# Chains of dependent operations split into single steps, in a new hand-written order, in an SSD and SwiGLU kernel on one core

## The chip, the cores and the metric

The kernel runs on one core of one Trainium2 chip. The core has five engines with an instruction queue each: TensorE (PE, with its weight loads shown as PEld), VectorE (DVE), ScalarE (ACT), GpSimd (POOL) and SyncE (SP, which here issues nearly all DMAs). Every engine works through its own queue in order; between engines an instruction waits on a semaphore. The metric is the device time of the program in microseconds (us), median over runs; lower is better.

## The reference

Two stages, one behind the other, all in fp32:

```python
# stage 1: x (4 batches, 8 heads, 768 steps, 32), a (4, 8, 768), B and C (4, 8, 768, 16); chunks of 32
log_a = np.log(np.clip(a, 1e-06, 1.0))
cum = np.cumsum(la, axis=-1)                       # within a chunk
L = np.exp(cum[:, :, :, None] - cum[:, :, None, :]) * causal
y_intra = (C B^T * L) x
y_inter = (C state) * exp(cum)
state = exp(sum(la)) * state + sum_j B_j x_j * exp(cum[-1] - cum_j)
# stage 2: y reshaped to 3072 tokens x 256
xn = x / sqrt(mean(x * x) + 1e-06) * rms_g
g = xn @ w_gate                                    # 256 -> 1536
silu = g / (1 + exp(-g))
val = xn @ w_val
out = (silu * val) @ w_out                         # 1536 -> 256
```

The weights of the second stage come as 64-bit floats and are turned into 32-bit ones on the chip.

## The kernel before, in words

The 3072 tokens are worked in six blocks of 512, and each block's first stage in two pairs of 128-token chunks (the pairs 0 to 11). While TensorE does the second stage of one block, the other engines prepare the first stage of the next ones. Block 0 has code of its own, since its first stage and the conversion of the weights have to be done before anything else can run.

*First stage.* A logarithm of `a`, sums of it by matmuls (`sums_of_logs`, L402; `row_sums`, L1161), and `three_parts` (L411 to L417), which splits a row of sums into three bf16 parts in four steps on DVE, each reading the one before. `mask` (L474) opens a PSUM pair with a mask, `sums` (L488, L495) adds the sums to it, and `decay` takes the exponential on ACT. `products` (L606, L613) makes `g`, C times B; `decayed` (L646 to L658) multiplies the two on DVE into `L`. `additions` (L678) gives what each chunk adds to the state, and `states` (L692 to L702) carries the state along on DVE: one masked copy for each half, then a chain of steps of 128 x 64 elements. `outputs` (L719 to L750) makes `y`. `squares` (L791, L802), `norm_sums` (L830, L834), `norm_roots` (two steps on ACT, a logarithm and an exponential) and `norm_apply` (L861, L865) do the RMS norm; `taken_out` (L812 to L821) copies `y` out of PSUM. For later pairs the decays come from rows spread by DMA (`spread`, L514), a subtraction (L520, DVE or POOL), an exponential on ACT and a triangular cut on POOL (`causal`, L507).

*Weights.* They come in 18 pieces. `fetch` issues the DMA (L182, L185) into one of six buffers; `power` (three steps on ACT, each reading the one before) makes the exponent, `mantissa` (two steps on DVE, L234 and L237) the fraction, and `weight` (L243, DVE) multiplies them into `wgv` or `wo`.

*Second stage.* For the later products gate and value come by a Strassen-like scheme of seven products (`product_gv`, L965) over sums of weights (`combine_w`, L934) and of tokens (`combine_x`, L942); ACT takes a part sum out of PSUM (`taken_gv`, the copy `p`, L971), DVE adds (`total_gv`, `c`, L977), ACT applies the silu (L215, a helper through which all activations go), DVE or POOL multiplies (`hide_gv`, `hid`, L990). The output product has a scheme of twenty products (`product_o`, L1086) over sums (`sum_h`, `combine_wo`) and totals (`total_o`, L1117, L1113). Block 0 starts with plain products (`products_early`, L889; `products_gv`, L879; `normed`, L900; `hidden`, L912; `first_projection`, L997).

Silu and the exponential or logarithm live in two tables of ACT. `functions` (L202 to L209) issues a table load each time the needed table differs from the one that is in.

*The order.* There is no scheduler: one string, `order` (from L1284), names every step of the program, as `block:kind.arguments`. The steps are emitted as the string has them, and each lands at the end of its engine's queue. `/n` picks a PSUM pair, `*n` puts n filler matmuls ahead. A step that is a chain in its helper, as `pow`, `man`, `parts`, `S`, `sq`, `yt`, `rs`, `norm`, `ex`, goes into its queue as a whole.

Of the kernel before, what the change touches and what calls it, by code (L numbers as in the profile page):

```python
# [20 lines left out]
def kernel(  # L21
# [195 lines left out]
    def power(k):  # L217
        words16, (lo, hi), dst, shape = fetched[k]
        n = shape[1] * shape[2]
        e = cvt.tile([P, n], FP32, tag="e", name="e", bufs=4)  # L220
        k16 = e.bitcast(I16)[:, n:2 * n].rearrange("p (a b) -> p a b", a=shape[1])
        g = e.rearrange("p (a b) -> p a b", a=shape[1])
        b16 = e.bitcast(I16)[:, 0:n].rearrange("p (a b) -> p a b", a=shape[1])
        activation(out=k16, in_=words16, func=AF.Relu, scale=1.0 / 16, bias=kinks[:, 0:1])
        activation(out=g, in_=k16, func=AF.Prelu, scale=-1.0, bias=kinks[:, 1:2],
                             alpha=2.0 ** -20)
        activation(out=b16, in_=g, func=AF.Prelu, scale=-2.0 ** 27, bias=kinks[:, 2:3],
                             alpha=2.0 ** -20)
        parts[k, "e"] = b16.bitcast(BF16)

    def mantissa(k):
        words16, (lo, hi), dst, shape = fetched[k]
        m = cvt.tile(shape, I32, tag="m", name="m")
        nc.vector.tensor_scalar(out=m, in0=hi, scalar1=0xFFFFF, scalar2=0x100000,  # L234
                                op0=ALU.bitwise_and, op1=ALU.bitwise_or)
        parts[k, "f"] = f = m.bitcast(FP32)
        nc.vector.scalar_tensor_tensor(out=f, in0=lo.bitcast(U32), scalar=2.0 ** -32, in1=m,  # L237
                                       op0=ALU.mult, op1=ALU.add)
# [54 lines left out]
    def whole_chunks():  # L293
        nc.vector.memset(chunk_ones, 0.0)
        for u, r in enumerate(halves):
            nc.vector.memset(chunk_ones[r, u], 1.0)
# [12 lines left out]
    def of_quarters():  # L309
        nc.vector.tensor_scalar(out=three, in0=part[:, 3:4], scalar1=-1.0, scalar2=1.0,  # L310
                                op0=ALU.mult, op1=ALU.add)
        nc.vector.tensor_scalar_add(later_part, part[:, 0:1], -1.0)
        nc.vector.tensor_scalar(out=third_part, in0=part[:, 2:3], scalar1=-1.0, scalar2=None,
                                op0=ALU.mult)
# [4 lines left out]
    def from_middle():  # L319
        nc.vector.tensor_copy(out=mid, in_=upto)  # L320
        nc.vector.tensor_scalar_add(mid[0:HC], mid[0:HC], -1.0)

    def from_middles():
        nc.gpsimd.tensor_copy(out=mid, in_=upto)
        for r in halves:
            half_of = slice(r.start, r.start + HC // 2)
            nc.gpsimd.tensor_scalar(out=mid[half_of, r], in0=mid[half_of, r], scalar1=-1.0,
                                    scalar2=None, op0=ALU.add)
        minus_mid()

    def mask16():
        for r in halves:
            nc.vector.tensor_copy(out=never16[r], in_=never[r, r])

    def kinks_of_powers():
        for k, v in enumerate((1152.0 - 7.5 / 16, 256.0, -1792.0 * 128.0)):
            nc.vector.memset(kinks[:, k:k + 1], v)
# [68 lines left out]
    def three_parts(k):  # L406
        r_ps = ps.pop(("r", k))
        room = nrm.tile([P, 4, P], FP32, tag="lead1", name="room", bufs=1)
        first, second = [room[:, k].bitcast(BF16).rearrange("p (s m) -> p s m", s=2)
                         for k in range(2)]  # L410
        nc.vector.tensor_copy(out=first, in_=r_ps)  # L411
        rest = room[:, 2:4]
        nc.vector.scalar_tensor_tensor(out=rest, in0=first, scalar=later_part, in1=r_ps,
                                       op0=ALU.mult, op1=ALU.add)
        nc.vector.tensor_copy(out=second, in_=rest)
        rows[k] = row = const.tile([P, 2, P], BF16, name="row%d" % k)
        nc.vector.scalar_tensor_tensor(out=row, in0=second, scalar=third_part, in1=rest,  # L417
                                       op0=ALU.mult, op1=ALU.add)
# [31 lines left out]
    def chunk_decays():  # L450
        activation(out=full.rearrange("p g h -> p (g h)"), in_=ps.pop("c"), func=AF.Exp)
        nc.gpsimd.tensor_tensor(out=fsel, in0=full,
# [52 lines left out]
    def causal(L):  # L505
        for r in halves:
            nc.gpsimd.affine_select(out=L[r], in_=L[r], pattern=[[0, L.shape[1]], [1, HC]],  # L507
                                    compare_op=ALU.is_ge, fill=0.0, base=0, channel_multiplier=-1)

    def spread(g):  # L510
        b, c = divmod(g, NC)
        o = (c * BH + b * NH) * HC
        for u, r in enumerate(halves):
            nc.sync.dma_start(out=pair_tile(g)[r].rearrange("p h m -> p (h m)"),  # L514
                              in_=rowv[u, o:o + NH * HC].partition_broadcast(HC))
# [8 lines left out]
    def exponential(g):  # L524
        L = pair_tile(g)
        activation(out=L, in_=L, func=AF.Exp)
        causal(L)

    def decays(g):
        subtract(g)  # L530
        exponential(g)
# [153 lines left out]
    def states(p):  # L685
        A_ps = ps.pop(("A", p))
        b, c0, chunks = chunks_of(p)
        new = ssd.tile([P, 2, 2, 2, D], FP32, tag="A", name="A")
        for u in range(2):
            n = sum(v == u for i, v in chunks)  # L690
            if n:
                nc.vector.tensor_tensor(  # L692
                    out=new[:, u, 0:n], in0=A_ps[u][:, 0:n],
                    in1=tmask.unsqueeze(1).unsqueeze(3).to_broadcast([P, n, 2, D]), op=ALU.mult)
        for i, u in chunks:
# [87 lines left out]
    def squares(p):  # L783
        blk, half = divmod(p, 2)
        if half == 0:
            sqs[blk] = nrm.tile([P, 2, TB], FP32, tag="sq", name="sq", bufs=1)
        n, tk, cols = columns_of_y(p)
        if p < 2:
            sq2 = sqs[blk][:, 1].rearrange("p (k m) -> p k m", k=2)
            activation(out=sq2, in_=ps["y", p][:, :, 0:256], func=AF.Square)  # L790
            nc.gpsimd.tensor_tensor(out=sqs[blk][:, 0, tk], in0=sq2[:, 0], in1=sq2[:, 1],  # L791
                                    op=ALU.add)
# [3 lines left out]
        for k in range(2):  # L796
            activation(out=dst[:, k, 0], func=AF.Square,
                                 in_=y[2 * k][:, cols].rearrange("p (j m) -> p j m", j=n))
        activation(
            out=dst[:, :, 1], func=AF.Square,  # L800
            in_=ps["y pair", p][:, :, cols].rearrange("p k (j m) -> p k j m", j=n))
        nc.gpsimd.tensor_tensor(out=sqs[blk][:, 0, tk], in0=sqs[blk][:, 0, tk],  # L802
                                in1=sqs[blk][:, 1, tk], op=ALU.add)

    def taken_out(p, copy):
        blk, half = divmod(p, 2)
        if half == 0:
            yts[blk] = nrm.tile([P, 2, TB], FP32, tag="yt", name="yt", bufs=1)
        n, tk, cols = columns_of_y(p)
        if p < 2:  # L810
            for t in range(2):
                nc.vector.tensor_scalar(out=yts[0][:, t, tk], in0=ps["y", p][:, t, 0:256],  # L812
                                        scalar1=gcol[:, t:t + 1], scalar2=None, op0=ALU.mult)
# [3 lines left out]
        for k in range(2):  # L817
            copy(out=dst[:, k, 0], in_=y[2 * k][:, cols].rearrange("p (j m) -> p j m", j=n))
        pair = ps["y pair", p][:, :, cols].rearrange("p k (j m) -> p k j m", j=n)
        for r, there in zip(halves, halves[::-1]):  # L820
# [672 lines left out]
```

## Time and profile before

| what | us |
|---|---|
| median of 3 runs | 392.02 |
| the three runs | 392.02, 392.39, 391.25 |
| profiled execution: its span | 389.5 |
| busy of it: PE, DVE, ACT, POOL | 383.3, 289.8, 226.4, 152.0 |

The times hold the whole program. The span reaches from the first to the last instruction of one profiled execution. Its own time outside the span isn't listed; to the median of the runs it lacks 2.5 us. In the rows shown below, a time such as 37.87 is the start in us from the beginning of the span, followed by the duration; then the engine, the line of the kernel, the operation, output and inputs by the names of the program, and their shapes. A bracket at the end gives the idle time ahead of the instruction and what ended it. TensorE's granted clock is 1.00 over the whole span.

### The profile page before, as it was taken

To read this page: it belongs to the slowest core of one execution; us is meant where nothing else is said; L and a number is where in the kernel's file an instruction comes from. 1 tells how busy PE (TensorE), PEld (TensorE's weight loads), DVE (VectorE), ACT (ScalarE), POOL (GpSimd) and SP (SyncE) were. 2 spreads that over 40 slices of the span, in tenths; PEclk is the share of its full clock that TensorE was granted. 3 is DMA by queue.
4 is the path that set the end of the run, shared out by engine and by line. 5 is a ranking of instruction groups with operands and counts; after the bars stand their busy time and mean duration, and the time that the engine had idled before them with its cause. 6 is when DMAs were issued, how large, how long until landed. Compare 5 with 4: busy or idle time off the path is not lost.

```text
span 389.5 us, 9637 instructions
## 1 busy us (share of the span) xinstructions
PE 383.3 (98%) x3805; PEld 329.8 (85%) x3805; DVE 289.8 (74%) x612; ACT 226.4 (58%) x471; POOL 152.0 (39%) x168
## 2 busy tenths in 40 slices
PE   8999999999999999999999999999999999999996
PEld 5676478788888999888899988899888899988995
DVE  6999999997976988669594765768374577454684
ACT  2899979988767262665865234763444571345420
POOL 5022045523693455343577701364611234212231
PEclk9999999999999999999999999999999999999999
DMA  8978984474073414634336112000100001000001
GB/s 107 241 153 259 240 195 147 120 157 42 3 101 86 50 13 94 145 42 96 70 78 81 27 42 42 2 15 22 56 3 2 2 12 50 29 0 0 2 0 56
DMA packets 109940, 28.05 MB, mean 72 GB/s; under 512 B 94824, under 2 KB 103752, under 8 KB 109896
## 3 DMA queue, kind: packets, MB, share of 16 engines
q1 hardware_dynamic: 107816, 27.31, 32.8%
q8 instruction: 30, 0.49, 0.5%
q10 hardware_dynamic: 2080, 0.13, 0.4%
q14 instruction: 14, 0.11, 0.1%
HBM read 23.69 MB, written 3.74 MB: 70 GB/s over the span
## 4 chain that ended last, share of the span: by engine, by line
PE 87%; DVE 9%; issue 2%; ACT 1%; DVEq 0%; ACTq 0%
PE gate L965 29%; PE o L1086 23%; PE val L965 21%; PE o L997 5%; PE y L750 3%; PE g L613 1%; DVE wgv L243 1%; DVE m L237 1%; DVE m L234 1%; DVE hid L912 1%; PE g L606 1%; PE e L474 1%; PE y L678 1%; DVE L L652 1%; ACT yt L821 0%
## 5 line engine op out<-in xcount | busy, mean ns | idle before, releaser
L977 DVE TENSOR_TENSOR c<-val,p 128x512 f32<-128x512 f32 x99 | 67.4, 686 | 45.1 <-PE val L965 33.3
L971 ACT COPY p<-gate 128x512 f32<-128x512 f32 x99 | 56.8, 581 | 57.5 <-PE gate L965 55.4
L965 PE MATMUL gate<-tx,wgv 128*128 128x256 f32 x264 | 65.9, 381 | 0.0
L215 ACT ACTIVATE c<-c 128x256 f32<-128x256 f32 x99 | 40.0, 415 | 38.7 <-DVE c L977 38.4
L990 POOL TENSOR_TENSOR hid<-c 128x256 f32<-128x256 f32 x31 | 24.7, 800 | 87.1 <-ACT c L215 83.1
L965 PEld LDWEIGHTS gate<-tx,wgv 128*128 128x128 f32 x264 | 49.2, 190 | 7.3 <-ACT p L971 0.7
L1117 DVE TENSOR_TENSOR ob<-ob,o 128x128 f32<-128x128 f32 (+1 forms) x90 | 24.2, 298 | 21.7 <-PE o L1086 16.9
L990 DVE TENSOR_TENSOR hid<-c 128x256 f32<-128x256 f32 x68 | 34.5, 521 | 6.9 <-ACT c L215 6.7
L1086 PE MATMUL o<-two,hid 128*128 128x128 f32 x280 | 36.5, 276 | 0.1
L1086 PEld LDWEIGHTS o<-two,hid 128*128 128x128 f32 x280 | 34.5, 192 | 1.1 <-DVE hid L990 0.4
L965 PE MATMUL val<-xn,wgv 128*128 128x256 f32 x132 | 33.7, 381 | 0.0
L965 PE MATMUL val<-tx,sw 128*128 128x256 f32 x132 | 33.5, 380 | 0.0
L965 PE MATMUL val<-xn,sw 128*128 128x256 f32 x132 | 33.3, 381 | 0.0
L965 PE MATMUL gate<-tx,sw 128*128 128x256 f32 x132 | 33.1, 381 | 0.0
L965 PE MATMUL gate<-xn,wgv 128*128 128x256 f32 x132 | 32.8, 381 | 0.0
L507 POOL TENSOR_SCALAR_AFFINE_SELECT L<-L 64x512 f32<-64x512 f32 x32 | 23.6, 737 | 18.6 <-ACT L L215 17.4
L965 PEld LDWEIGHTS val<-xn,wgv 128*128 128x128 f32 x132 | 24.8, 190 | 3.5
L965 PEld LDWEIGHTS val<-tx,sw 128*128 128x128 f32 x132 | 24.8, 190 | 3.5 <-issue 0.2
L965 PEld LDWEIGHTS gate<-tx,sw 128*128 128x128 f32 x132 | 24.7, 190 | 3.5 <-ACT p L971 0.2
L965 PEld LDWEIGHTS gate<-xn,wgv 128*128 128x128 f32 x132 | 24.3, 190 | 3.4 <-DVE hid L912 0.3
L965 PEld LDWEIGHTS val<-xn,sw 128*128 128x128 f32 x132 | 24.4, 190 | 3.2 <-issue 0.2
L215 ACT ACTIVATE e<-e,kinks 128x512 f32<-128x512 int16 (+1 forms) x36 | 26.0, 722 | 1.2
(203 smaller groups left out, 717.0 us busy)
## 6 DMA issues: line engine op xcount, KB each, us to landing
L<-rowd SPq DMA_DIRECT2D x32, 128.0 KB, 3.4
xr<-in_x_dram SPq DMA_DIRECT2D x24, 128.0 KB, 3.2
wr<-in_moe_w_out_dram SPq DMA_DIRECT2D x6, 512.0 KB, 5.6
out_dram<-ob SPq DMA_DIRECT2D x24, 128.0 KB, 1.8
wr<-in_moe_w_gate_dram SPq DMA_DIRECT2D x5, 512.0 KB, 5.8
wr<-in_moe_w_val_dram SPq DMA_DIRECT2D x5, 512.0 KB
br<-in_B_dram SPq DMA_DIRECT2D x23, 64.0 KB, 2.6
dT<-rowe SPq DMA_DIRECT2D x10, 128.0 KB
```

Of the source, the lines that this page charges most:

```text
L215: nc.scalar.activation(**operands)
L234: nc.vector.tensor_scalar(out=m, in0=hi, scalar1=0xFFFFF, scalar2=0x100000, op0=ALU.bitwise_and, op1=ALU.bitwise_or)
L237: nc.vector.scalar_tensor_tensor(out=f, in0=lo.bitcast(U32), scalar=2.0 ** -32, in1=m, op0=ALU.mult, op1=ALU.add)
L507: nc.gpsimd.affine_select(out=L[r], in_=L[r], pattern=[[0, L.shape[1]], [1, HC]], compare_op=ALU.is_ge, fill=0.0, base=0, channel_multipli ...
L750: nc.tensor.matmul(out=y[2 * k + u][rows, (2 * n + i) * HC:(2 * n + i + 1) * HC], start=(k, u, rows.start) not in opened, stop=True, skip_ ...
L965: nc.tensor.matmul(out=dst[:, half[w]], lhsT=lhsT, rhs=rhs, start=(k in (1, 2, 5) and w == 0), stop=True, skip_group_check=True)
L971: nc.scalar.copy(out=t, in_=Xs[j])
L977: nc.vector.tensor_tensor(out=t, in0=Zs[j], in1=a, op=ALU.add)
L990: engine.tensor_tensor(out=hid[:, 2 * j + c // 10 - 1, c % 10 - 1], in0=u, in1=src[:, half[1]], op=ALU.mult)
L997: nc.tensor.matmul(out=o, lhsT=hid[:, f, k // 2, (k % 2) * P:(k % 2 + 1) * P], rhs=wo[:, f], start=opens, stop=(f == NF - 1), skip_group_c ...
L1086: nc.tensor.matmul(out=Os[blk, b][:, place * P:(place + 1) * P], lhsT=hidden_or_sum(u)[:, g], rhs=rhs, start=(blk, b) not in opened, stop= ...
L1117: nc.vector.tensor_tensor(out=o, in0=o, in1=src, op=ALU.add if what[0] == "+" else ALU.subtract)
```

## The change

Every helper that emitted a chain takes one argument more, a stage, and emits one operation per call: `power` (three stages), `mantissa` (two), `three_parts` (four), `states` (split into `new_states`, step `Sn`, and one call for each chunk), `squares`, `taken_out`, `norm_roots`, `norm_apply`, `normed`, the early products, `spread` by halves, and several small steps of the start. The cut on POOL leaves the exponential and becomes a step of its own, `ca`. In block 0 `norm_apply` becomes two operations of 128 x 512 in place of one of 128 x 1024. Everything that is computed stays as it was. The bookkeeping of which PSUM pair is held (`held`, `leave`) is left out.

The string `order` is written anew from the first step to the end of block 3, with smaller moves in blocks 4 and 5, in such a way that two-operand operations of DVE do not stand beside operations of POOL. Which steps POOL does and which DVE does is nearly the same. In the new order ACT's table changes 28 times in place of 22.

```diff
-    def power(k):
+    def power(k, stage):
         words16, (lo, hi), dst, shape = fetched[k]
         n = shape[1] * shape[2]
-        e = cvt.tile([P, n], FP32, tag="e", name="e", bufs=4)
+        if stage == 0:
+            parts[k, "pow"] = cvt.tile([P, n], FP32, tag="e", name="e", bufs=4)
+        e = parts[k, "pow"]
...
-        activation(out=k16, in_=words16, func=AF.Relu, scale=1.0 / 16, bias=kinks[:, 0:1])
-        activation(out=g, in_=k16, func=AF.Prelu, scale=-1.0, bias=kinks[:, 1:2],
-                             alpha=2.0 ** -20)
-        activation(out=b16, in_=g, func=AF.Prelu, scale=-2.0 ** 27, bias=kinks[:, 2:3],
-                             alpha=2.0 ** -20)
-        parts[k, "e"] = b16.bitcast(BF16)
+        if stage == 0:
+            activation(out=k16, in_=words16, func=AF.Relu, scale=1.0 / 16, bias=kinks[:, 0:1])
+        elif stage == 1:
+            activation(out=g, in_=k16, func=AF.Prelu, scale=-1.0, bias=kinks[:, 1:2],
+                       alpha=2.0 ** -20)
+        else:
+            activation(out=b16, in_=g, func=AF.Prelu, scale=-2.0 ** 27, bias=kinks[:, 2:3],
+                       alpha=2.0 ** -20)
+            parts[k, "e"] = b16.bitcast(BF16)
...
-    def mantissa(k):
+    def mantissa(k, stage):
         words16, (lo, hi), dst, shape = fetched[k]
-        m = cvt.tile(shape, I32, tag="m", name="m")
-        nc.vector.tensor_scalar(out=m, in0=hi, scalar1=0xFFFFF, scalar2=0x100000,
-                                op0=ALU.bitwise_and, op1=ALU.bitwise_or)
-        parts[k, "f"] = f = m.bitcast(FP32)
-        nc.vector.scalar_tensor_tensor(out=f, in0=lo.bitcast(U32), scalar=2.0 ** -32, in1=m,
-                                       op0=ALU.mult, op1=ALU.add)
+        if stage == 0:
+            parts[k, "m"] = m = cvt.tile(shape, I32, tag="m", name="m")
+            nc.vector.tensor_scalar(out=m, in0=hi, scalar1=0xFFFFF, scalar2=0x100000,
+                                    op0=ALU.bitwise_and, op1=ALU.bitwise_or)
+        else:
+            m = parts.pop((k, "m"))
+            parts[k, "f"] = f = m.bitcast(FP32)
+            nc.vector.scalar_tensor_tensor(out=f, in0=lo.bitcast(U32), scalar=2.0 ** -32, in1=m,
+                                           op0=ALU.mult, op1=ALU.add)
...
-    def causal(L):
-        for r in halves:
-            nc.gpsimd.affine_select(out=L[r], in_=L[r], pattern=[[0, L.shape[1]], [1, HC]],
-                                    compare_op=ALU.is_ge, fill=0.0, base=0, channel_multiplier=-1)
+    def causal(g, u):
+        L, r = pair_tile(g), halves[u]
+        nc.gpsimd.affine_select(out=L[r], in_=L[r], pattern=[[0, L.shape[1]], [1, HC]],
+                                compare_op=ALU.is_ge, fill=0.0, base=0, channel_multiplier=-1)
...
     order = """
-        0:warm 0:a 0:set 0:bc.0 0:ident 0:bc.1 0:bc2.1.1 0:ones 0:zeros 0:ident16 0:whole 0:kinks
-        0:idle.7 0:gcol 0:x.0 0:never 0:after 0:fetch.0 0:fetch.1 0:x.1 0:whole16 0:mask.0.0/0
-        0:part 0:hmask 0:upto 0:mid 0:mids 0:part2 0:aT 0:mask.1.1/2 0:la0 0:log4.0.4 0:upto2 0:r.0
-        0:fetch.2 0:head 0:sel 0:middles 0:after2 0:fetch.3 0:log4.4.2 0:log4.6.2 0:bc.3 0:tmask
-        0:parts.0 0:log 0:c*2 0:cx 0:mask.0.1/1 0:turn.0 0:Tb.0 0:T.0 0:d 0:dx 0:sums.0.1 0:sums.0.0
-        0:exp.0.1 0:never16 1:exps 0:exp.0.0 0:turn.1 0:scale.1.0 0:scale.1.1 0:last.1 0:cc
...
-        0:early.1.0/1 0:early.1.1 0:dT.3 0:man.4 0:table.1 0:x.2 0:norm.1 0:man.5 0:Td.3 0:silu.0
...
-        0:spread.8 0:ms.1 0:take.6.5 0:P.7.5 0:rs.1 0:pow.13 0:sub.9 0:o.0/2 0:o.1 0:sub.10 0:man.13
-        0:fetch.14 0:hidg.21.4 0:take.7.5 0:wt.13 1:cwp.2.0 0:hidgp.22.3 0:cwp.0.3 0:C.22.5 0:P.4.5
...
+        0:warm 0:a 0:set 0:bc.0 0:ident 0:bc.1 0:bc2.1.1 0:ones 0:zeros 0:fetch.0 0:upto 0:mid.0
+        0:mean 0:upto2 0:part 0:whole.0 0:part2.0 0:never 0:hmask 0:part2.2 0:x.0 0:fetch.1 0:idle.7
+        0:kinks.0 0:kinks.1 0:mid.1 0:part2.1 0:ident16 0:whole16 0:mask.1.1/2 0:mask.0.0/0 0:aT
+        0:la0 0:mask.0.1/1 0:after 0:after2 0:mids 0:log4.0.4 0:r.0 0:never16.0 0:parts.0.0
+        0:parts.0.1 0:whole.1 0:middles.0 0:middles.1 0:middles.2 0:log 0:d 0:middles.3 0:dx 0:tmask
+        0:head 0:sel 0:kinks.2 0:whole.2 0:c*2 0:cx 0:ch 0:turn.1 0:Tt.1.0 0:scale.1.1 0:parts.0.2
+        0:T.1 0:Tt.1.1 1:exps 0:parts.0.3 0:sums.0.1 0:exp.0.1 0:turn.0 0:scale.0.0 0:T.0 0:Tb.0
...
+        0:pow.4.1 0:Tt.3.0 0:early.1.1/1 0:Tt.2.1 0:Tt.2.0 0:early.1.0 0:norm.1.0 0:T.3 0:norm.1.1
+        0:Td.3 0:man.5.0 0:gate.2/0 0:scale.3 0:pow.4.2 0:scale.2 0:wt.4 0:cw.0.0 0:gg.2/1 0:pow.5.0
+        0:pow.5.1 0:fetch.7 0:pow.5.2 0:pow.7.0 0:man.5.1 0:L.2.0 0:tx.0.2 0:L1.2.2 0:man.7.0 0:wt.5
...
+        1:silu.11.0 1:silu.22.0 1:hidp.22.0 1:P.3.1 1:C.12.1 0:table.0 1:silu.21.0 0:ex.10
...
```

596 lines of the change are left out of this document (320 added, 276 removed).

## The prediction

> **What bounds the kernel now.** I read the totals first, then the busy time by stage, then the waits of TensorE, and last the timeline of single engines where those pointed.
>
> The totals, the shares of the chain that ended last, and stages that I cut where the character of the work changes (length of the stage, then busy time and count of each engine, the granted clock, and the share and rate of the DMA engines):
>
> ```profile
> span 389.5 us, 9637 instructions
> PE 383.3 (98%) x3805; PEld 329.8 (85%) x3805; DVE 289.8 (74%) x612; ACT 226.4 (58%) x471; POOL 152.0 (39%) x168
> PE 87%; DVE 9%; issue 2%; ACT 1%; DVEq 0%; ACTq 0%
> ```
> ```profile
> 0.00:9.00 9.00, 7.76 (x33) 5.11 (x33) 5.62 (x28) 2.65 (x6) 4.53 (x17) 1.00 0.84 94
> 9.00:22.00 13.00, 12.35 (x220) 8.50 (x220) 12.30 (x28) 11.04 (x19) 1.59 (x2) 1.00 0.92 212
> 22.00:53.50 31.50, 31.38 (x349) 19.39 (x348) 30.64 (x64) 29.85 (x48) 4.45 (x5) 1.00 0.88 222
> 53.50:56.00 2.50, 2.00 (x29) 1.45 (x35) 2.30 (x7) 2.25 (x9) 1.01 (x2) 1.00 1.02 154
> 56.00:75.00 19.00, 18.98 (x257) 15.46 (x240) 18.35 (x40) 16.84 (x36) 9.82 (x13) 1.00 0.42 140
> 75.00:385.50 310.50, 309.97 (x2938) 279.20 (x2938) 219.53 (x446) 163.82 (x357) 130.65 (x132) 1.00 0.24 46
> 385.50:389.50 4.00, 0.85 (x8) 0.66 (x6) 1.10 (x4) 0.00 (x0) 0.00 (x0) 0.99 0.19 66
> ```
>
> From 75 to 385.5 us, four fifths of the span, TensorE is busy 309.97 of 310.50 us and DVE and ACT have room. The change alters no matmul, so there is nearly nothing to win there. Before 75 us three engines are full at once: between 22 and 53.5 us TensorE 31.38, DVE 30.64 and ACT 29.85 of 31.50. The chain that ended last runs through DVE from 17 to 53 us, which is its 9%. So a quicker DVE helps in that stretch only as far as TensorE really waits in it. Its waits between 9 and 75 us (total, times, longest):
>
> ```profile
> PE y L719 <- DVE S L700: 0.5, 1, 0.5
> PE g L613 <- ACT sq L215: 0.5, 1, 0.5
> ```
>
> A busy PE is not PE at its peak, so I looked for hidden stalls, groups that last longer than like groups:
>
> ```profile
> 36.57 1.16 PE L613 MATMUL g<-T 32*64 32x128 f32 x32
> 55.70 0.70 PE L613 MATMUL g<-T 32*64 32x128 f32 x32 [0.50 <-ACT sq L215]
> 71.06 3.67 PE L997 MATMUL o<-wo,hid 128*128 128x256 f32 x16
> 74.75 1.13 PE L965 MATMUL gate<-tx,wgv 128*128 128x256 f32 x4
> ```
> ```profile
> 75.88 3.45 PE o L997 x16
> ```
>
> The same 32 matmuls of `g` take 1.16 us at 36.57 and 0.70 at 55.70: 0.46 hidden. The 16 of `o` need 3.45 in the chain, but from 71.06 to the next group at 74.75 pass 3.69: 0.24. With the 0.5 at 55.70 that is 1.2 us seen between 22 and 75 us; the small stretches of the gate products about 50 to 55 and 66 to 71 us (a tenth or two each) may double it. I take 2.3 us as the most that a better order can give back there.
>
> **The sum, part by part.** It is made against the profiled execution, span 389.5. The median of the runs is 392.02, 2.5 above the span, and all runs lie in 391.25 to 392.39; I add the sum to the median, so that what lies around the span stays in.
>
> *Dependent pairs on DVE.* Rows of DVE (start, duration):
>
> ```profile
> 37.87 0.68 DVE L652 TENSOR_TENSOR L<-g,L 128x512 f32<-128x512 f32 x1
> 38.47 0.68 DVE L243 SCALAR_TENSOR_TENSOR wgv<-m,e 128x512 f32<-128x512 f32 x1
> 39.18 0.43 DVE L234 TENSOR_SCALAR m<-wr 128x512 int32<-128x512 int32 x1
> 39.64 0.69 DVE L237 SCALAR_TENSOR_TENSOR m<-wr,m 128x512 f32<-128x512 uint32 x1
> ```
>
> The weight at 38.47 needs nothing of its predecessor and starts 0.08 before that one ends (37.87 + 0.68 = 38.55). L237 needs L234 and starts 0.03 after it ends (39.18 + 0.43 = 39.61). A step that follows its own input thus costs 0.11 us more, and the change takes it apart by one foreign step. By the order of the two kernels, DVE has 23 such neighbours among the instructions that before issues from 15 to 50 us, and 5 after; 18 × 0.11 = 2.0 us of DVE time. [...]
>
> On ACT it is the same, and there are two table loads among these rows:
>
> ```profile
> 69.47 0.57 ACT L971 COPY p<-gate 128x512 f32<-128x512 f32 x1
> 70.06 1.28 ACT L209 ACT_TABLE_LOAD   x1
> 71.35 0.37 ACT L215 ACTIVATE r<-ms,eps 128x128 f32<-128x128 f32 x1
> 71.97 0.75 ACT L215 ACTIVATE e<-wr,kinks 128x512 int16<-128x512 int16 x1
> 72.75 1.48 ACT L215 ACTIVATE e<-e,kinks 128x512 f32<-128x512 int16 x2
> 74.13 0.56 ACT L971 COPY p<-gate 128x512 f32<-128x512 f32 x1
> 74.72 1.28 ACT L207 ACT_TABLE_LOAD   x1
> 76.01 0.38 ACT L215 ACTIVATE u<-gate 128x256 f32<-128x256 f32 x1
> ```
>
> The second step of `power` starts 0.03 after the first ends (71.97 + 0.75 = 72.72); the copy at 74.13 starts 0.10 before its predecessor ends (74.23). In the same stretch ACT has 19 such pairs before, 10 after: 9 × 0.13 = 1.2 us. DVE and ACT feed each other, so the two do not add; the bound of both is TensorE's 2.3 us.
>
> *Rows of POOL.* A two-operand step of DVE beside one of POOL is slower:
>
> ```profile
> 33.32 1.10 DVE L237 SCALAR_TENSOR_TENSOR m<-wr,m 128x512 f32<-128x512 uint32 x1
> 32.28 1.59 POOL L942 TENSOR_TENSOR tx<-xn,tx 128x256 f32<-128x256 f32 x2
> ```
>
> 1.10 against 0.69: 0.41. The new order puts one-operand steps there, or leaves one there that is no shorter; I take −0.4 (0 to −0.7) of DVE time, beneath the same bound.
>
> *What the new order asks earlier.* The first output product that needs weights from `wo` comes 4.3 us of matmul work earlier in the new order, while the DVE steps ahead of that weight shrink by 3.4 us only, by the durations of the rows of before. That takes 0.9 back. And before it ACT binds in both kernels: in the rows above, the copy `p` that ends at 74.69 stands behind the table load at 70.06, and the product that needs it starts at 74.75. That order is kept. So of the 2.3 us I count −1.4 as won between 22 and 75 us (0 to −2.3).
>
> *Start-up.* Rows of PE and of DVE:
>
> ```profile
> 2.79 1.01 PE L474 MATMUL e<-whole,ident 128*128 128x512 bf16 x2
> 3.60 0.52 PE L347 MATMUL aT<-ident,a_sb 96*128 96x96 f32 x2
> 3.92 1.06 PE L474 MATMUL e<-whole,ident 128*128 128x512 bf16 x2
> 7.62 0.60 PE L474 MATMUL e<-whole,ident 128*128 128x512 bf16 x2
> ```
> ```profile
> 6.32 0.43 DVE L411 CAST room<-r_ps 128x256 bf16<-128x256 f32 x1 [0.83 <-PE r_ps L402]
> ```
>
> Before, `aT` stands between the two early mask groups. After, both stand ahead of it, and they need `ident16` and `whole16`, which DVE now makes later, so `aT`, the logarithms and `room` come about 1.1 later (one mask group, 1.01 to 1.06, which at this early time takes twice the 0.60 of 7.62). The DVE steps that stood behind `room` are pulled ahead of it, so half comes back: +0.6, with 0 and +1.3 as ends. This lies on the path, since 9 to 22 us is where TensorE loses most (12.35 of 13.00 even by its busy time), all of it waiting for the first states. The new order also has the first `fetch` ahead of the first `x` on SP's queue, and the loads of B and C behind the first row store; the first `xr` is needed at 16.9 us, issued before at 6.4, so a neighbour's issue is hidden; were it not, it is within the +1.3.
>
> ```profile
> 6.37 1.09 SPq L150 DMA_DIRECT2D xr<-in_x_dram  x2
> ```
> ```profile
> 16.92 0.70 PE L678 MATMUL A_ps<-xr,Bd 128*32 128x64 f32 x32
> ```
>
> *Six more table loads.* The order of ACT has 28 against 22, since exponentials and silus of blocks 0 to 2 alternate one by one. Six by 1.28 and the lost overlap of 0.1 make 8.3 us of ACT. They all fall after 75 us, where ACT is busy 163.82 of 310.50. The cover is that idle time and the copies `p` issued a product or two ahead. I take 0; if the cover were gone, +8.3. (The Trainium skill, "ScalarE: Activation LUTs", section "What ACT_TABLE_LOAD costs", puts a switch at about 1.28 us of loading and as much again for draining, together 2.7; six of these would be an estimated 16 us of ACT. Here the load begins 0.02 after the copy of 69.47 ends and the next step 0.01 after the load: no second half.)
>
> *Later waits.* One row stands for four small stalls, which I read from the timeline about 146, 150, 193 and 382 us at 0.3 to 0.4 each:
>
> ```profile
> 382.51 1.16 PE L1086 MATMUL o<-sw,hid 128*128 128x128 f32 x8 [0.38 <-DVE ob L1117]
> ```
>
> In the new order what these wait for stands further ahead: −0.6 (0 to −1.1; an order this new may also make stalls, +0.6). The end (4.0 us from the last products to the last store) is the same order in both: 0. One more DVE instruction, the `norm_apply` of block 0 as two halves, costs 0.1, and lets the first half be used sooner: 0.
>
> Sum: −1.4 + 0.6 + 0 − 0.6 = −1.4; 392.02 − 1.4 = **390.6 us**. With the good ends of all terms −2.3 + 0 − 1.1 = −3.4, 388.6.
>
> **The rivals.**
> - *Slower, by the table loads* (0.22). Place: ACT's queue in blocks 0 to 2, where the change splits three groups of exponentials. A pair of loads, 2.6 us, stands ahead of a copy `p`, and a product waits for it. For: about 74.7 us just this costs 0.24 with two table loads 3.4 us apart. Against: 146.7 us of ACT idle in that stage. It decides once the copy was due less than 2.6 us ahead of its product; at half a pair each (1.3), three pairs make +3.9, so 392.0 − 1.4 + 3.9 = 394.5; at a fifth, 391.6. The start-up at its bad end would add 0.7 to that.
> - *The split does nothing, or ACT binds anyway* (0.26). If a dependent neighbour costs nothing of its own, or the rows about 74.7 us set the pace, then DVE's gain is not passed on: 0 instead of −1.4, later −0.6, start-up +0.6: 392.0. For: ACT busy 29.85 of 31.50. Against: the 0.46 at 36.57 waits for `T`, a DVE step in a row of pairs.
> - *The forecast* (0.52), 389.3 to 391.0.
>
> The bound for faster or slower is 0.3%, 1.2 us, about what the spread of three runs can tell from nothing. Faster 0.53, same 0.25, slower 0.22. The range leaves out the last 0.2 of the good ends and takes in the slower rival at half a pair each: 388.8 to 394.6.
>
> **What would show it.** In the changed kernel: `room` at 7 us or later instead of 6.32; no neighbouring L234 and L237 rows with the 0.03 gap; the `g` group that took 1.16 at 0.70; TensorE's last product about 1.5 us sooner, the gain standing by 75 us; 28 table loads with no wait of TensorE on a copy `p` behind one. I am wrong if waits of PE on ACT appear between 80 and 200 us (first rival), if the start of the second pair's states slips by over 1 us, or if the stage before 75 us is no shorter although its DVE pairs are gone (second rival).

## The result, and the profile after

The changed kernel takes 393.9 us (median of 4 runs, 393.21 to 394.45) against 391.66 of the kernel before (4 runs, 391.25 to 392.39): ratio 1.0061, 95% interval 1.0042 to 1.0081. It is slower by about 2.2 us, where 1.4 us faster was forecast. Measured once more, on the chip of three of the experiments, the same kernel gave 393.31 against 391.10, ratio 1.0045 (1.0031 to 1.0060).

The profile after, its totals, the shares of the chain that ended last, and the stages cut as in the prediction:

```profile
span 392.7 us, 9639 instructions
PE 384.4 (98%) x3805; PEld 328.8 (84%) x3805; DVE 282.5 (72%) x613; ACT 234.0 (60%) x477; POOL 147.9 (38%) x168
PE 84%; SPq 5%; DMA 3%; ACT 3%; DVE 3%; issue 1%; POOL 0%; DVEq 0%; POOLq 0%; ACTq 0%
```
```profile
0.00:9.00 9.00, 6.99 (x29) 3.68 (x29) 4.54 (x27) 2.33 (x4) 3.82 (x16) 1.00 0.85 123
9.00:22.00 13.00, 12.72 (x174) 9.06 (x174) 11.04 (x24) 9.92 (x20) 1.06 (x1) 1.00 0.89 190
22.00:53.50 31.50, 31.50 (x393) 18.96 (x391) 30.25 (x67) 28.14 (x46) 5.58 (x7) 1.00 0.85 204
53.50:56.00 2.50, 1.19 (x6) 1.06 (x6) 2.47 (x9) 2.40 (x6) 0.71 (x1) 1.00 0.60 60
56.00:75.00 19.00, 19.00 (x257) 15.54 (x256) 17.05 (x41) 17.71 (x39) 8.36 (x12) 1.00 0.62 161
75.00:385.50 310.50, 308.84 (x2917) 276.54 (x2917) 213.31 (x437) 173.20 (x364) 127.71 (x133) 1.00 0.24 46
```

The waits of TensorE in it, over the whole span (total, times, longest):

```profile
PE gate L1002 <- ACT p L1008: 1.3, 1, 1.3
PE idle L359 <- DVE warm L385: 1.1, 1, 1.1
PE o L1034 <- DVE wo L252: 1.1, 1, 1.1
PE e L501 <- DVE whole L401: 0.5, 1, 0.5
PE gate L1002 <- DVE xn L897: 0.4, 1, 0.4
```

DVE has what the change set out to give it: its busy time falls from 289.8 to 282.5 us (283.9 in a second profile, that of `after_again`), with one instruction more. ACT's rises from 226.4 to 234.0, close to the six table loads. But the time belongs to TensorE. Up to 385.5 us its idle time, from the two sets of stages, grows by 0.77 in 0 to 9 us (7.76 and 6.99 busy of 9.00), by 0.81 in 53.5 to 56 (2.00 and 1.19 of 2.50) and by 1.13 from 75 on (309.97 and 308.84 of 310.50), and falls by 0.37 from 9 to 22, by 0.12 from 22 to 53.5 and by 0.02 from 56 to 75: together +2.2. Its busy time is 1.1 longer for the same matmuls (384.4 and 383.3). Behind 385.5 us the idle time falls by 0.1. That makes up the difference of the two spans, 3.2. These are two single executions, and the profiled one of the changed kernel is the slowest of its four; the medians differ by 2.2.

Each place has its rows. The start, on TensorE and on DVE:

```profile
3.29 1.86 PE L501 MATMUL e<-whole,ident 128*128 128x512 bf16 x4 [0.50 <-DVE whole L401]
4.95 0.52 PE L364 MATMUL aT<-ident,a_sb 96*128 96x96 f32 x2
5.27 1.06 PE L501 MATMUL e<-whole,ident 128*128 128x512 bf16 x2
6.43 0.67 PE L419 MATMUL r_ps<-mids,early_ones 128*128 128x256 f32 x2
```
```profile
7.14 0.42 DVE L434 CAST room<-r_ps 128x256 bf16<-128x256 f32 x1 [0.75 <-PE r_ps L419]
```

The masks begin at 3.29 in place of 2.79, because `whole16` is made later on DVE; `aT` starts at 4.95 in place of 3.60; `room` at 7.14 in place of 6.32.

About 54 us, on ACT and on TensorE:

```profile
52.81 0.75 ACT L215 ACTIVATE e<-wr,kinks 128x512 int16<-128x512 int16 x1
53.59 0.72 ACT L215 ACTIVATE e<-e,kinks 128x512 f32<-128x512 int16 x1
54.22 0.56 ACT L1008 COPY p<-gate 128x512 f32<-128x512 f32 x1
```
```profile
54.83 1.13 PE L1002 MATMUL gate<-tx,sw 128*128 128x256 f32 x4 [1.31 <-ACT p L1008]
```

Two steps of `power` for weight piece 11 stand in ACT's queue ahead of the first copy `p`. TensorE has nothing else to do there, and waits 1.31 us.

About 83 us, on SP's queue, ACT, DVE and TensorE:

```profile
73.06 0.34 SPq L883 DMA_DIRECT2D roots<-r  x1
73.50 0.39 SPq L182 DMA_DIRECT2D wr<-in_moe_w_out_dram  x1
```
```profile
79.91 0.79 ACT L215 ACTIVATE e<-wr,kinks 128x512 int16<-128x512 int16 x1 [1.90 <-DMA wr<-in_moe_w_out_dram]
82.24 0.69 DVE L252 SCALAR_TENSOR_TENSOR wo<-m,e 128x512 f32<-128x512 f32 x1 [0.96 <-ACT e L215]
82.99 3.72 PE L1034 MATMUL o<-wo,hid 128*128 128x256 f32 x16 [1.08 <-DVE wo L252]
```

The load of weight piece 14 stands behind the store of the roots in SP's queue, lands at about 79.8, and the output product that needs it waits 1.08 us. In the kernel before it stands behind that store too (72.09 and 72.54), and ACT takes its data at 76.29 without a wait. So the place behind the store is not the whole cause; from issue to use pass 6.4 us here and 3.8 there, and what makes the landing later is open.

### The profile page after: what moved, and what is told of

Its sections match the earlier page's. It is cut to its first block, busy times and chain, and to the rows that moved or that the text cites. A ratio compares the mean times of both kernels' runs of the same rounds, so it can differ in the third digit from the quotient of the medians.

```text
span 392.7 us, 9639 instructions
## 1 busy us (share of the span) xinstructions
PE 384.4 (98%) x3805; PEld 328.8 (84%) x3805; DVE 282.5 (72%) x613; ACT 234.0 (60%) x477; POOL 147.9 (38%) x168
## 4 chain that ended last, share of the span: by engine, by line
PE 84%; SPq 5%; DMA 3%; ACT 3%; DVE 3%; issue 1%; POOL 0%; DVEq 0%; POOLq 0%; ACTq 0%
PE gate L1002 27%; PE o L1123 19%; PE val L1002 19%; PE gate L914 4%; PE o L1034 4%; SPq L133 3%; PE y L777 2%; PE gate L926 2%; DMA wr<-in_moe_w_out_dram 2%; ACT e L215 1%; PE g L635 1%; PE e L501 1%; SPq L541 1%; PE g L628 1%; DMA roots<-r 1%
## 5 line engine op out<-in xcount | busy, mean ns | idle before, releaser
L1027 POOL TENSOR_TENSOR hid<-c 128x256 f32<-128x256 f32 x31 | 23.0, 748 | 80.1 <-ACT c L215 71.9
L1123 PE MATMUL o<-two,hid 128*128 128x128 f32 x280 | 38.5, 276 | 0.1
L1027 DVE TENSOR_TENSOR hid<-c 128x256 f32<-128x256 f32 x68 | 32.1, 486 | 8.3 <-ACT c L215 7.8
L1123 PEld LDWEIGHTS o<-two,hid 128*128 128x128 f32 x280 | 35.5, 192 | 1.4 <-issue 0.4
L534 POOL TENSOR_SCALAR_AFFINE_SELECT L<-L 64x512 f32<-64x512 f32 x32 | 22.2, 701 | 18.8 <-ACT L L215 17.6
```

Source lines behind the costliest of these rows:

```text
L1027: engine.tensor_tensor(out=hid[:, 2 * j + c // 10 - 1, c % 10 - 1], in0=u, in1=src[:, half[1]], op=ALU.mult)
L1123: nc.tensor.matmul(out=Os[blk, b][:, place * P:(place + 1) * P], lhsT=hidden_or_sum(u)[:, g], rhs=rhs, start=(blk, b) not in opened, stop= ...
```

## The experiments

All kernels are timed beside the kernel before on the same chip. The ratios are to that; the changed kernel itself stands at 1.0061 and 1.0045 in two measurements. Four chips were used: one for b_split, h_ab, f_take and f_fetch, one for h_ba, s_aT, s_g and x_ba, one for after_again, p_pairs, s_r0 and b_loads, one for s_nine and x_best. Orders are given in the step names of the changed kernel. In the hybrids the steps are divided into two sets, and each set keeps the order that one of the two kernels has for it.

| kernel | ratio to before | interval |
|---|---|---|
| b_split: before's order, chains written out | 1.0001 | 0.9989 to 1.0014 |
| h_ab: start of after, rest of before | 1.0079 | 1.0063 to 1.0095 |
| h_ba: start of before, rest of after | 1.0003 | 0.9993 to 1.0013 |
| after_again: after, once more | 1.0045 | 1.0031 to 1.0060 |
| f_take: after, one copy earlier | 1.0038 | 1.0022 to 1.0053 |
| f_fetch: after, one load earlier | 1.0041 | 1.0029 to 1.0054 |
| x_ba: h_ba with both moves | 0.9992 | 0.9982 to 1.0002 |
| s_aT: after, aT first | 1.0040 | 1.0028 to 1.0053 |
| s_r0: after, first sums ahead of the third mask | 1.0035 | 1.0019 to 1.0050 |
| s_g: after, other PSUM pair | 1.0063 | 1.0051 to 1.0075 |
| s_nine: first 8 us of before, rest of after | 1.0037 | 1.0024 to 1.0049 |
| x_best: x_ba, aT first | 1.0041 | 1.0029 to 1.0053 |
| p_pairs: before, weight pairs taken apart | 1.0030 | 1.0020 to 1.0040 |
| b_loads: before, six table loads more | 1.0029 | 1.0017 to 1.0040 |

**The steps alone (b_split).** The helpers of after, and every chain of before's string written out:

```diff
-        0:S.0 0:S.1 0:pow.0 0:wt.0
+        0:Sn.0.1 0:S.0.0 0:S.0.1 0:Sn.1.1 0:S.1.0 0:S.1.1 0:pow.0.0 0:pow.0.1 0:pow.0.2 0:wt.0
...
```

> The order of before, each chain written out as its single steps one behind the other, in the helpers of after; the one instruction more (the apply of block 0 as two halves) is in it. My theory (three waits of TensorE that the new order makes: start-up, the copy p about 54 us, a late weight piece about 82 us) expects the time of before, 391.7 +- 0.6, since no instruction changes its neighbours. Rival (the single steps themselves cost, by tiles held longer or more waits on semaphores): 393 or more.

1.0001: the helpers and the one instruction more cost nothing that can be measured. What the change does, the new order does.

**The start, both ways (h_ab, h_ba).** The steps up to `y` of the second pair from one kernel, the rest from the other. h_ba against after begins so:

```diff
-        0:warm 0:a 0:set 0:bc.0 0:ident 0:bc.1 0:bc2.1.1 0:ones 0:zeros 0:fetch.0 0:upto 0:mid.0
+        0:warm 0:a 0:set 0:bc.0 0:ident 0:bc.1 0:bc2.1.1 0:ones 0:zeros 0:ident16 0:whole.0 0:whole.1
...
```

> The steps up to the y of the second pair in the order of after, all later steps in the order of before. Theory: the start-up of after puts TensorE 1.2 us further back by 30 us and this is kept to the end, so 392.9 (+1.2 against before), range +0.8 to +1.9. Rival (what is lost in the start is absorbed by the slack that DVE and ACT have behind it): 391.7, within 0.4 of before.

> The steps up to the y of the second pair in the order of before, all later steps in the order of after: the start of before with the rest of after. Theory (the start of after costs 2.3 us of TensorE's progress by 30 us, and the rest of its order gains about 0.7 on before's in spite of its two waits): 0.5 to 1.0 us faster than before. Rival (the start only uncovers what the rest of the order loses anyway: the late copy p and the late weight piece set the time): within 0.5 us of after, 2 us slower than before.

h_ab is 0.8% slower than before (3.1 us at 391), h_ba the same as before. The intervals of h_ba and of after do not touch: putting before's start back gives after about 1.6 us (1.0045 to 1.0003), or 2.3 by the first measurement (1.0061), and that is nearly all that the change costs. In size I was wrong twice: h_ab costs more than the 1.2 expected, and h_ba gains nothing on before. For h_ab the trace shows why. Before and h_ab issue the same 3805 matmuls; where both have issued the same set of them, the start of the next one can be compared. h_ab is 1.4 us behind before at 19.3 us, 2.8 at 26.0, just past the seam, and 2.8 at the end; after, with the same start, is 1.9 behind at 28.6. So about 1 us of its loss comes where the start of after meets the rest of before. For h_ba one reason can be seen: the waits of h_ba's TensorE hold the 1.3 us on the copy `p` in full, where before waits 0.5 for `sq`:

```profile
PE gate L1002 <- ACT p L1008: 1.3, 1, 1.3
PE y L746 <- DVE S L727: 0.5, 1, 0.5
PE ms L860 <- POOL sq L820: 0.3, 1, 0.3
```

It has no wait on `wo`. That is not because of the earlier start, since the product that needs the load comes earlier by the same time; the load is taken 5.2 us after its issue (71.72 to 76.92), in place of 6.4 in after.

**One copy, one load (f_take, f_fetch, x_ba).**

```diff
-        0:P.1.3 0:P.2.3 0:pow.11.0 0:pow.11.1 0:take.1.3
+        0:P.1.3 0:P.2.3 0:take.1.3 0:pow.11.0 0:pow.11.1
```
```diff
-        0:rs.1.2 0:cw.1.2 1:S.1.1 0:sub.9 0:silug.22.3 1:S.1.2 0:hidgp.12.3 0:o.1 0:man.13.1 0:fetch.14
+        0:fetch.14 0:rs.1.2 0:cw.1.2 1:S.1.1 0:sub.9 0:silug.22.3 1:S.1.2 0:hidgp.12.3 0:o.1 0:man.13.1
```

> The order of after with one step moved: the copy p of the first part sum (take.1.3) ahead of the two ACT steps pow.11.0 and pow.11.1. Theory: the wait of TensorE of 1.3 us at 54.8 us shrinks below 0.3 and the end comes 0.9 to 1.3 sooner, 392.8 against 393.9. Rival (ACT is full there, the two moved steps make the next copy or the weight late by as much, so the wait turns up behind): 393.9, no change.

> The order of after with one DMA moved: the load of weight piece 14 ahead of the store of the roots (rs.1.2) on SP's queue. Theory: it is issued when its buffer is free, about 71.4 us in place of 73.5, the wait of TensorE on wo of 1.1 us at 83 us goes, 392.8 against 393.9. Rival (the transfers share the same queues, or the roots come later and xn of block 1 becomes late): 393.9 or more.

> The start of before with the rest of after, and in that rest both single moves: take.1.3 ahead of pow.11.0, and the load of weight piece 14 ahead of the store of the roots. Theory (three separate losses that add): 2.0 to 2.7 us faster than before, about 388.6. Rival (with an earlier start other waits take the places of these two): at most 1 us faster than before.

Each move does in the trace what it should. With the copy first, TensorE's next product starts without a wait, and of 1.3 us only a wait of 0.33 for the second copy is left:

```profile
53.33 1.13 PE L1002 MATMUL gate<-tx,sw 128*128 128x256 f32 x4
56.52 1.13 PE L1002 MATMUL gate<-tx,wgv 128*128 128x256 f32 x4 [0.33 <-ACT p L1008]
```

With the load ahead of the roots the wait on `wo` is gone. The times are less clear: 1.0038 and 1.0041 lie between the two measurements of after, and their intervals overlap that of 1.0045, so a gain of a single move is seen in the rows and not proven in the time. For the copy the traces show what becomes of it. TensorE issues its matmuls in the same order in after and f_take; the first product behind the copy starts 1.51 us sooner in f_take, the next that needs a copy 1.01 sooner, and the output product at 73.04 only 0.27. x_ba against h_ba does the same: 0.61 behind, then 0.81 ahead at 52.2 us, then 0.41 behind again at 71.7. The gain is given back within 20 us, for the most part inside groups of matmuls and not in waits that the list names. Another part is that the wait on `wo` is not the same in every execution: 1.1 in the profile of after, 0.2 in that of after_again, 0.6 in f_take, none in s_aT and s_r0, where the order around it is that of after. The load is taken 4.9 to 6.4 us after its issue in these executions. Both moves together on h_ba give 0.9992, 0.4 us better than h_ba; neither from h_ba nor from before is that a clear difference. So the theory of three losses that add (2.0 to 2.7 us faster than before) fell; its rival (the time is lost again behind) fits.

**Where the start loses it (s_aT, s_r0, s_g, s_nine, x_best).**

```diff
-        0:mask.1.1/2 0:mask.0.0/0 0:aT 0:la0 0:mask.0.1/1
+        0:aT 0:la0 0:mask.0.0/0 0:mask.1.1/2 0:mask.0.1/1
```
```diff
-        0:mask.1.1/2 0:mask.0.0/0 0:aT 0:la0 0:mask.0.1/1 0:after 0:after2 0:mids 0:log4.0.4 0:r.0
+        0:mask.0.0/0 0:aT 0:mask.1.1/2 0:la0 0:after 0:after2 0:mids 0:log4.0.4 0:r.0 0:mask.0.1/1
```
```diff
-        0:g.0.1/1 0:man.0.0 0:L.0.1 0:bc.2 0:rowe.1 0:sums.1.1 0:exp.1.1 0:last.0 0:last.1 0:mask.1.0/0
-        0:man.0.1 0:Tl.0 0:log4.4.2 0:g.0.0/1 0:L.0.0
+        0:g.0.1/1 0:g.0.0/0 0:man.0.0 0:L.0.1 0:L.0.0 0:bc.2 0:rowe.1 0:sums.1.1 0:exp.1.1 0:last.0
+        0:last.1 0:mask.1.0/1 0:man.0.1 0:Tl.0 0:log4.4.2
```

> The order of after with the transposition aT and the clipping la0 ahead of the two early masks on TensorE. Theory (the masks ahead of aT delay the whole chain of logarithms): 0.8 to 1.3 us faster than after. Rival (another step, the PSUM pair that g.0.0 waits for, sets the start): no change against after, 2.3 us slower than before.

> The order of after with TensorE's first steps in the sequence of before: one mask, aT, the other mask, the sums r.0, and only then the third mask. Theory (in after the first sums stand behind aT and three masks at the slow rate of the start, 1.3 us later): r_ps starts 0.7 to 1.0 us sooner, the end comes 0.7 to 1.5 sooner than after. Rival (r_ps is not on the path, the DVE steps ahead of T are): no change against after.

> The order of after with the second product of the first pair (g.0.0) on PSUM pair 0 right behind the first, its product with L right behind the other, and the mask of the second pair on pair 1, as before has it. In after g.0.0 waits until the first L step has freed pair 1, and L.0.0 starts 2.5 us behind L.0.1 (16.44 and 13.91). Theory: the first y comes 1 to 1.5 us sooner and so does the end, 0.8 to 1.5 us faster than after. Rival (the masks ahead of aT are the whole delay, TensorE does the same work in another order here): no change against after.

s_g changes nothing (1.0063): the PSUM pair is not it. s_aT and s_r0 are a little below after (1.0040 and 1.0035 against 1.0045 and 1.0061), with intervals that overlap that of 1.0045. In s_r0 the first sums start at 5.46 in place of 6.43, but by 9 us only 0.5 of this is left, and at 206 us the wait for `xn` is 1.06 in place of 0.44. s_aT is a weak test, as its trace shows: `aT` comes at 3.14, but three masks then stand between it and the first sums, which start at 6.05, only 0.4 earlier than in after.

s_nine takes the steps up to the three parts of the first sums, about 8 us, from before:

```diff
-        0:warm 0:a 0:set 0:bc.0 0:ident 0:bc.1 0:bc2.1.1 0:ones 0:zeros 0:fetch.0 0:upto 0:mid.0
+        0:warm 0:a 0:set 0:bc.0 0:ident 0:bc.1 0:bc2.1.1 0:ones 0:zeros 0:ident16 0:whole.0 0:whole.1
...
```

> The steps up to the three parts of the first sums (the first 8 us) in the order of before, everything behind them in the order of after. Theory (the start of after loses its 1.3 us within the first 9 us, by masks ahead of the first sums and small DVE steps ahead of theirs, and nothing more up to the y of the second pair): 1.1 to 1.9 us faster than after, within 0.5 us of before. Rival (the loss is in the steps from 9 to 24 us, as the PSUM pair of g.0.0 or the order of the states): no more than 0.6 us faster than after.

1.0037. Together with h_ba (1.0003) it divides the start: 0.0034, or 1.3 us, is lost by the order between about 8 and 24 us, and 0.0008 to 0.0024, 0.3 to 0.9 us, by the first 8. The second part is not clear of noise by the times, since the intervals of s_nine and after_again overlap. The traces, compared at the same matmul, agree with a division: after is 0.8 behind s_nine from 9 us on, and s_nine 1.0 behind h_ba from 24 us on, to which the wait on `wo` (0.8 in s_nine) comes later. Neither my theory (all in the first 9 us) nor its rival holds alone.

Where s_nine loses it between 9 and 24 us is not in a wait of TensorE: 9 to 22 us are 12.81 us busy there and 12.35 in h_ba. Both have issued the same 251 matmuls when the first product of the weights starts, at 21.63 in h_ba and at 23.08 in s_nine. Groups that stand together in h_ba stand apart in s_nine (the first two rows are h_ba's):

```profile
14.47 1.16 PE L628 MATMUL g<-T 32*128 32x256 f32 x16
16.47 0.70 PE L700 MATMUL A_ps<-xr,Bd 128*32 128x64 f32 x32
```
```profile
16.25 0.43 PE L700 MATMUL A_ps<-xr,Bd 128*32 128x64 f32 x16
18.25 0.43 PE L700 MATMUL A_ps<-xr,Bd 128*32 128x64 f32 x16
18.61 1.13 PE L628 MATMUL g<-T 32*128 32x256 f32 x8
```

Sixteen matmuls of `g` side by side take 1.16 us, eight alone 1.13. Counted from each start to the next, the 32 of `g` take 2.60 us in h_ba and 3.64 in s_nine and in after, the 32 of `A_ps` 0.52 and 0.96. This is about as much as s_nine loses, but that it is the cause is argued and not shown: in s_g the first two groups of `g` stand together again, and TensorE idles longer instead (2.98 us up to the first product of the weights, against 2.22 in after), and no run puts `g.1.1` and `g.1.0`, or the two halves of `A`, side by side in the order of after.

x_best moves `aT` ahead in the start of x_ba, and the second mask behind the first sums:

```diff
-        0:mask.0.0/0
+        0:aT 0:mask.0.0/0 0:la0 0:log4.0.4
...
-        0:aT 0:mask.1.1/2 0:la0 0:log4.0.4 0:upto2 0:r.0
+        0:upto2 0:r.0 0:mask.1.1/2
```

> The start of before with the rest of after, both single moves in it (take.1.3, load of piece 14), and the start mended once more: aT ahead of the first mask, the second mask behind the first sums. Theory (the first sums are on the path, and they come 0.4 us sooner): 0.3 to 0.5 us faster than the same kernel without this mending (0.9992), so 0.5 to 1.0 us faster than before. Rival (the a values arrive by DMA too late for an earlier aT, or TensorE stays slow for longer if it idles there): within 0.4 us of before.

It is 1.9 us slower than x_ba (1.0041 against 0.9992) and 1.6 slower than before, more than both theories allow. Compared with x_ba at the same matmul, it is 1.3 us behind by 8.7 us and stays so up to 144 us: all is lost in the start. Its rows on TensorE:

```profile
3.51 1.06 PE L501 MATMUL e<-whole,ident 128*128 128x512 bf16 x2
5.41 1.22 PE L419 MATMUL r_ps<-mids,early_ones 128*128 128x256 f32 x2 [0.83 <-POOL mids L381]
6.42 1.06 PE L501 MATMUL e<-whole,ident 128*128 128x512 bf16 x2
7.70 1.37 PE L469 MATMUL full_ps<-la,early_ones 128*128 128x192 f32 x4
9.05 0.59 PE L501 MATMUL e<-whole,ident 128*128 128x512 bf16 x2
```

The first sums did not come sooner: `aT` waits 0.39 us for the values of `a` by DMA, as the rival had it, and the sums wait 0.83 us for `mids` from POOL, which the mask had covered. And the matmuls behind still run at the slow rate of the start: the mask at 6.42 takes 1.06 us, the one at 9.05 takes 0.59. More on this below.

**Pairs alone, loads alone (p_pairs, b_loads).** In before's order, the steps of `power` and `mantissa` moved by one place; and in before's order, six table loads put in:

```diff
-        0:yt.0.0 0:yt.0.1 0:man.1.0 0:man.1.1 0:wt.1
+        0:yt.0.0 0:man.1.0 0:yt.0.1 0:man.1.1 0:wt.1
...
-        0:table.1 0:silu.0 0:pow.4.0 0:pow.4.1
+        0:table.1 0:pow.4.0 0:silu.0 0:pow.4.1
...
```
```diff
         0:ex.10
+        0:table.0
...
         0:ex.11
+        0:table.0
...
         1:ex.1
+        0:table.0
```

> The order of before with the steps of power and mantissa of the weight pieces 0 to 13 moved by one place, so that a foreign step stands between dependent ones; nothing else is moved. Dependent neighbours fall by 10 on DVE and by 22 on ACT up to about 75 us. Theory of my forecast (the pairs cost 0.11 to 0.13 each on the path): DVE gains 1.1 us, ACT 2.8, TensorE's waits of 1.2 to 2.3 us in that stretch shrink, 0.5 to 1.3 us faster than before. Rival (TensorE has too little to wait for there, or a dependent step costs no more than a foreign one): within 0.4 us of before.

> The order of before with six table loads more, three pairs, set between neighbouring exponentials of blocks 1 and 2 as the new order has them; nothing else is moved. Theory (8.3 us of ACT that lie in its idle time): within 0.4 us of before. Rival (a pair of loads stands ahead of a copy p that TensorE waits for): 1.0 to 3.9 us slower than before, with waits of PE on ACT between 95 and 160 us.

p_pairs is 0.3% slower, where 0.5 to 1.3 us faster was expected. The stretch from 22 to 53.5 us, in b_split and in p_pairs:

```profile
22.00:53.50 31.50, 31.37 (x349) 19.30 (x348) 30.71 (x67) 29.60 (x48) 5.61 (x6) 1.00 0.90 223
```
```profile
22.00:53.50 31.50, 30.47 (x347) 18.48 (x346) 30.55 (x65) 27.52 (x46) 4.55 (x5) 1.00 0.88 222
```

ACT is busy 27.52 in place of 29.60 us, with two instructions fewer in the window; over the whole span it is 224.3 in place of 226.6 for the same 471 instructions. So the pairs do cost ACT time. DVE shows no such gain: 289.2 in place of 289.1, although of 17 pairs of `mantissa` that stood as neighbours 6 are left. And TensorE is busy less too, 30.47 in place of 31.37. It waits for steps that were pushed back by one place, among them:

```profile
16.68 0.43 PE L700 MATMUL A_ps<-xr,Bd 128*32 128x64 f32 x16 [0.44 <-ACT T L620]
17.55 0.43 PE L700 MATMUL A_ps<-xr,Bd 128*32 128x64 f32 x16 [0.44 <-ACT tok L1266]
52.02 1.99 PE L1002 MATMUL gate<-xn,wgv 128*128 128x256 f32 x8 [0.75 <-DVE hid L949]
```

b_loads is 0.3% slower as well, 1.1 us, and one wait makes it:

```profile
105.51 1.28 ACT L209 ACT_TABLE_LOAD   x1
106.81 0.63 ACT L215 ACTIVATE L<-L 128x512 f32<-128x512 f32 x1
107.45 1.28 ACT L207 ACT_TABLE_LOAD   x1
108.75 0.58 ACT L1008 COPY p<-gate 128x512 f32<-128x512 f32 x1
```
```profile
109.39 1.99 PE L1002 MATMUL gate<-tx,wgv 128*128 128x256 f32 x8 [1.45 <-ACT p L1008]
```

So the slower rival of the prediction is a real mechanism. Where it strikes, a pair costs what the rival put on it (1.45 against 1.3), but only one of three pairs strikes. In after it does not occur, though some of its 28 loads stand as close (135.1 and 136.7 us): its one wait on a copy `p` is not behind a load.

## Why the prediction was wrong, point by point

The matmuls that before and another kernel have both issued serve as milestones. The table has the start of the next matmul in before, and how much later it starts in the others:

| before, us | after | after_again | h_ba |
|---|---|---|---|
| 28.59 | 1.88 | 1.89 | 0.07 |
| 49.07 | 1.12 | 1.12 | −0.69 |
| 52.44 | 2.40 | 2.39 | 0.61 |
| 74.75 | 1.81 | 1.82 | 0.03 |
| 80.25 | 3.06 | 2.18 | 0.05 |
| 386.08, the last | 3.29 | 2.11 | −0.54 |

The sum had +0.6 for the start, −1.4 between 22 and 75 us and −0.6 later. The second profile of the changed kernel (after_again), a run at the median of its set, has +1.9 up to 28.59, −0.1 from there to 74.75 and +0.3 behind. All are single executions, and their starts alone can differ by 1 us (last section).

- *What bounds the kernel.* Right as far as it went: TensorE is at 98% before and after, and only what it waits for counts. The use of it was wrong. I bounded the gain between 22 and 75 us by TensorE's waits (2.3 us), and then took for certain that the waits that exist could only shrink. A new order can make new ones at any place, and this one made two, of 1.31 and 1.08 us.
- *Dependent pairs and rows of POOL, −1.4 between 22 and 75 us.* This is the step that failed: it measured −0.1. The stalls that it counted on did go. The 32 matmuls of `g` that took 1.16 us take 0.69, and the group that waited 0.50 for `sq` waits no more:

```profile
38.33 0.69 PE L635 MATMUL g<-T 32*64 32x128 f32 x32
58.48 0.69 PE L635 MATMUL g<-T 32*64 32x128 f32 x32
```

By 49 us the new order had won 0.8 back. What the sum had not was the price of the new places: the copy `p` behind two steps of `power` took 1.3 us away at 52 to 54 us. The wait for `sq` that is gone gave 0.6 back, and that leaves −0.1. A step that is set between two others to cover their gap delays what stands behind them. p_pairs shows this in its pure form: 2.3 us less busy time on ACT and 1.2 us slower. For DVE the 0.11 us for a pair did not show in its busy time there, so its 7.3 us less in after are not shown to come from the pairs; no run takes the rows of POOL alone.

- *Table loads, 0.* Right for this order: no wait on a copy `p` behind a load. Wrong as a statement on loads in general, as b_loads shows with 1.45 us for one packed group.
- *What the new order asks earlier, +0.9 within the −1.4.* Right in kind, though it falls at 80 us, behind that stretch. The output product that comes earlier in the order does wait for `wo`, though for piece 14 and its DMA, not for the steps of DVE. I treated SP's queue as covered; the load behind the roots takes 6.3 us to the landing in this execution (73.50 to 79.83 in the chain), 5.5 at most in after_again, where before it took at most 3.8 (72.5 to the use at 76.29).
- *Start-up, +0.6 (0 to +1.3).* The second step that failed. It was right in sign and in part of the mechanism, and too small. `room` at 7.14 is the "7 us or later" that I named as the sign. But the sum over the whole start is 1.6 us by h_ba against after_again, and up to 3.1 by h_ab; more than half of it lies between 8 and 24 us (s_nine), where I had counted on DVE steps pulled ahead of `room` to give half back. The sign that I had named for this case is there: the second pair's states, which began at 19.51, begin at 22.12, 2.6 us later.
- *Later waits, −0.6.* Half right: the wait of 0.38 at the end is gone, and one of 0.44 for `xn` at 207.64 is new. With the start of before the term came out (−0.6 behind 74.75 us in h_ba); in after the wait on `wo` and that for `xn` made it +1.5, in after_again +0.3.
- *The rivals.* None of the three was what happened. The slower one had the right kind of mechanism, a copy `p` behind other work in ACT's queue, with the wrong work in front: two steps of `power` that the change itself had set free to move there. (Its price at a fifth of a pair each is 392.2, not 391.6: 392.0 − 1.4 + 1.6.)

## What to carry to other kernels

When one engine is nearly always busy, price an edit of the order by the arrival of each input of that engine, one by one, and not by the busy time it saves on the others: here 7 us less on DVE came with 2 us more at the end. Chains that stand together lose about a tenth of a microsecond per link by the rows above, but they finish early; taking them apart lets foreign work in between, and with it into the latency of whatever TensorE needs next. The same holds for matmuls that ran side by side: apart, they can cost the busy engine more without a single wait. Look first at the first microseconds, and at single steps that stand ahead of a copy or a load that the busy engine will ask for.

## What the runs showed of the hardware that was not expected

TensorE starts at about half of its later rate (a mask of two matmuls takes 1.06 us, later 0.60), and when this changes differs by up to three microseconds between executions of the same order. The second early mask and the first sums in b_split, and the first sums in before, which issues the same matmuls:

```profile
3.93 0.73 PE L501 MATMUL e<-whole,ident 128*128 128x512 bf16 x2
5.10 0.67 PE L419 MATMUL r_ps<-mids,early_ones 128*128 128x256 f32 x2 [0.44 <-issue]
```
```profile
5.09 1.19 PE L402 MATMUL r_ps<-mids,early_ones 128*128 128x256 f32 x2
```

0.67 us in one execution, 1.19 in the other. In b_split the change falls within the mask at 3.93 (0.73 against 1.06 in before); in before the mask of two matmuls is at full rate only at 7.62 (0.60). TensorE is about 1 us further on by 8 us in b_split, and the spans differ by as much (388.5 and 389.5). This is as large as the effects that were looked for here, so a single profile of a start says little. In x_best, where TensorE idles for 0.39 us before `aT` and for 0.83 before the first sums, the slow rate lasts until about 8.8 us. The granted clock of the profile reads 1.00 in all of these stages, as in this one of x_best:

```profile
5.00:7.00 2.00, 1.59 (x4) 0.95 (x5) 1.06 (x5) 0.13 (x1) 0.64 (x2) 1.00 0.96 91
```

So the slow phase shows in the durations and not in that column. The Trainium skill, "TensorE: Matmul & The Clock Gate", "Part 1: The HAM clock gate", describes a half rate that ends after one busy window of about 3.4 us of a free-running counter. It puts the change at around 4 us into sustained matmuls, give or take 0.5 us between runs. Here the first matmul is at 1.11 us and the change comes about 3, 6 and (in x_best, with the gaps) 7.7 us later, so the spread in these runs, whose matmuls have gaps, is wider than the page's.
